# Ten of eleven f tiles of a gated feed-forward block's down product as 2x2 block products in seven, for half of the tokens

## The chip, the cores and the metric

The kernel runs on one core of one Trainium2 chip. The metric is the device time of one execution in microseconds. Engine names in the profile: PE is TensorE (PEld its weight loads), DVE is VectorE, ACT is ScalarE, POOL is GpSimd, SP the engine whose queue issues the transfers.

## The reference, cut to what matters

A transformer block with adaptive layer norm, linear attention and a bilinear feed-forward part, 2048 tokens of 512 features, all in float32:

```
h = layernorm(x) * (1 + ca) + sa
x = x + ga * linear_attention(h, wqkv) @ wo
h = layernorm(x) * (1 + cb) + sb          # 2048 x 512
g = h @ w_gate                            # 2048 x 1376
u = h @ w_up                              # 2048 x 1376
x = x + gb * ((g * u) @ w_down)           # w_down: 1376 x 512
```

The change is in the last three lines.

## The kernel before

The tokens are four chunks of 512. In the feed-forward part two chunks make a side: side 0 is chunks 0 and 1, side 1 is chunks 2 and 3. The 1376 columns of w_gate and w_up are eleven f tiles (ten of 128, the last of 96). The loop over `order` runs 22 blocks: all f tiles of side 0, and then all of side 1. The f tiles are in five groups, `groups`: four of two and a last of three.

A number is carried as two float32r parts, a high one and a low one (`split`: ScalarE copies the high part, another engine subtracts). A product then takes three matmuls: high by high, high by low, low by high. A float32r matmul loads 128x128 weights and streams up to 512 columns into one PSUM bank.

One block computes, for its f tile, gate and up of both chunks as a product of 2x2 blocks (chunks by halves of the features, halves of the features by gate and up) with seven products instead of eight, in Winograd's form. `block` (line 984) writes them in a fixed order with `times` (line 965): seven products of 6 matmuls of 512 columns, into four banks a, b, c and d that all blocks share. ScalarE's `copy` carries a partial sum from bank to bank between the products: after b has its product with s2, b goes to c; after c has its product with s3, c is copied into u3, which VectorE adds to d; the product with a22 then goes on top in c. At the end VectorE multiplies gate by up (`product_of`, line 994) and gets two tiles h, one for each chunk; `todo` holds the splits of these, which run in the next block behind its second product (`flush`). `at` is a table of work that the loop puts at named points between the products: a11, s1, s2, s3, pe, mid, s4. The engines run their instructions in the order in which the program issues them, and an instruction that waits holds all behind it on its engine. All transfers are issued on SP's queue, in order.

The right side of a block, `Right` (line 921), is loaded from w_gate and w_up, three blocks ahead; GpSimd makes the differences that the seven products need (`sums`), ScalarE the high parts and GpSimd the low parts (`high`, `lows`). It is made anew for each side. The left side of side 1 is prepared during side 0 and kept in DRAM (`aside`, `fetch`).

The down product (`down`, line 1039) of a group runs in the blocks of the next group. A job takes two token tiles (of the four of a chunk), and for each of them 3 matmuls of 512 columns for each f tile of the group, into a bank of the pool `ps_acc` (4 banks); VectorE adds the bank to the token tile in `xts` (line 1055). The jobs stand at the point pe, between the products with s3 and with a22; their adds are issued at s4. The jobs of the last group of side 1 have no block behind them: one job of four token tiles and four of one are issued after the last block, each add followed by the store of its tile of the output. w_down's rows are scaled by gb on VectorE (`scale_down`) and split (`split_down`).

All working tiles, 2 KB in each partition, are from one pool of 99 (`B`); the program's order decides which place a new tile gets, and whose last use it waits for.

Of the kernel before, what the change touches and what calls it, by code (L numbers as in the profile page):

```python
# [22 lines left out]
def tile_adaln_block(  # L23
# [41 lines left out]
    def f32(ap):  # L65
        return ap.bitcast(F32)
# [7 lines left out]
    def B(tag, shape=(P, D), dt=F32):  # L74

        return T(tiles, tag, shape, dt)
# [313 lines left out]
    sums = {}  # L390
# [522 lines left out]
    def fetch(stash, side, *names):  # L913
        for n in names:
            side[n] = []
            for k in range(KH):
                side[n].append(tuple(B("h", dt=F32R) for _ in range(2)))
                for part, x in enumerate(side[n][k]):
                    nc.sync.dma_start(f32(x), stash[n, k, part])

    class Right:
# [24 lines left out]
        def high(self):  # L946
            self.parts = []
            self.b11 = self.tile("w", F32R)
            nc.scalar.activation(self.b11[:, 0], self.up[:, 0], AF.Copy)  # L949
            for names, x in ((("t1", "t2"), self.t12), (("b21", "b22"), self.low), (("t3", "t4"), self.t34)):  # L950
                h = self.tile("w", F32R)
                nc.scalar.activation(h, x, AF.Copy)
                self.parts.append((names, x, h))

        def lows(self, on=None):
            sub = lambda out, x, y: (on or nc.gpsimd).tensor_tensor(out, x, f32(y), op=ALU.subtract)  # L956
            self.of = {"b11": (self.b11[:, 0], self.b11[:, 1])}
            sub(self.b11[:, 1], self.up[:, 0], self.b11[:, 0])
            for names, x, h in self.parts:
                l = self.tile("w", F32R)  # L960
                sub(l, x, h)
                for i, name in enumerate(names):
                    self.of[name] = (h[:, i], l[:, i])

    def times(ps, left, right, fresh):

        (bh, bl) = right
        for k in range(KH):
            ah, al = left[k]
            mm = lambda x, y, **kw: nc.tensor.matmul(ps, x[:, k], y, skip_group_check=True, **kw)  # L970
            mm(bh, ah, start=fresh and k == 0, stop=False)
            mm(bh, al, start=False, stop=False)
            mm(bl, ah, start=False, stop=k == KH - 1)

    def copy(out, x):
        nc.scalar.activation(out, x, AF.Copy)  # L976
# [4 lines left out]
        while todo:  # L981
            todo.pop(0)()

    def block(A, R, at={}, end=False):


        n, R = R.n, R.of
        a, b, c, d = (x[:n] for x in (abank, bbank, cbank, dbank))
        out = [None, None]

        def also(point):
            run(at.get(point, ()))

        def product_of(i, x, y):
            t = B("phi")
            nc.vector.tensor_tensor(t[:n], x, y, op=ALU.mult)  # L996

            def halves():
# [23 lines left out]
        nc.vector.tensor_tensor(c22[:n], d, u3[:n], op=ALU.add)  # L1022
# [12 lines left out]
        rest()  # L1035
        also("s4")
        return out

    def down(ch, hs, ds, js=range(NJ), last=False):
# [17 lines left out]
                    nc.sync.dma_start(ov[ch, j], xt)  # L1057
        return take

    def load_down(f):  # L1060
        f0, n = fts[f]
        return load(w_down[f0:f0 + n, :], "raw")

    def scale_down(d):
        nc.vector.tensor_tensor(d, d, gb[:d.shape[0]], op=ALU.mult)
# [3 lines left out]
    order = [(s, g, f) for s in range(2) for g in range(len(groups)) for f in groups[g]]  # L1069
    rights = {}  # L1070

    def right_load(n):
        if n < len(order):
            rights[n] = Right(order[n][2])

    def right_sums(n, on=None):
        if n < len(order):
            rights[n].sums(on)

    def right_split(n, on=None):  # L1080
        if n < len(order):
            rights[n].high()
            rights[n].lows(on)

    side, stash, lefts = {}, {}, {}

# [111 lines left out]
    }  # L1198

    before = None  # L1200
    for n, (s, g, f) in enumerate(order):
        first, final = f == groups[g][0], f == groups[g][-1]
        if first:
            if before is not None:
                down_jobs(*before)
            for x in groups[g]:
                raw_d[s, x] = load_down(x)
        at = {p: list(early.get((n, p), ())) for p in ("a11", "s1", "s2", "s3", "mid", "s4", "pe")}
        taken = []
        after = len(groups[g]) - groups[g].index(f)  # L1210
        for _ in range(-(-len(fillers) // after)):
            job = fillers.pop(0)
            at["pe"].append(lambda job=job: taken.append(job()))
            at["mid" if n + 1 == len(order) else "s4"].insert(0, lambda: taken.pop(0)())
# [12 lines left out]
        at["s3"] += [lambda n=n: right_load(n + 3)]  # L1227
        at["s4"] += [lambda n=n: right_sums(n + 2), lambda d=raw_d[s, f]: scale_down(d)]
        if n:
            at["s2"].insert(0, lambda s=order[n - 1][0], f=order[n - 1][2]: split_down(s, f))  # L1230
        if s == 0 and n == 9:
            after_side = {}
            at["pe"].append(lambda: fetch(stash, after_side, "a11", "a12"))
# [5 lines left out]
        hs[s, f] = block(side, rights.pop(n), at=at)  # L1239
# [11 lines left out]
_INS = ["A_x", "A_wqkv", "A_wo", "B_w_gate", "B_w_up", "B_w_down", "c", "w_mod"]  # L1251
# [24 lines left out]
```

## Time and profile before

| | us |
|---|---|
| median of 3 runs | 563.58 (562.93 to 564.28) |
| profiled execution, its own time | 561.47 |
| its span, first to last instruction | 559.8 |

| engine | busy us | share of the span | instructions |
|---|---|---|---|
| PE | 551.9 | 99% | 2544 |
| DVE | 379.8 | 68% | 648 |
| ACT | 294.2 | 53% | 531 |
| POOL | 207.4 | 37% | 226 |

Transfers read 43.12 MB from and wrote 13.63 MB to DRAM. The blocks of side 1 begin about 384 us from the span's start.

In the rows of the profile, a group is one line of the kernel on one engine: what it writes and reads, the tiles' sizes, the count, then busy time and the mean duration of one in ns, and the idle time before it with who ended it. A row of a timeline begins with the start and the duration in us. A row of a stretch has its bounds and length, then PE, PEld, DVE, ACT and POOL busy with their counts, the granted clock, the share of the transfer engines and GB/s. Matmuls overlap: their durations add up to more than the time they take.

### The profile page before, as it was taken

To read this page: it belongs to the slowest core of one execution; us is meant where nothing else is said; L and a number is where in the kernel's file an instruction comes from. 1 tells how busy PE (TensorE), PEld (TensorE's weight loads), DVE (VectorE), ACT (ScalarE), POOL (GpSimd) and SP (SyncE) were. 2 spreads that over 40 slices of the span, in tenths; PEclk is the share of its full clock that TensorE was granted. 3 is DMA by queue.
4 is the path that set the end of the run, shared out by engine and by line. 5 is a ranking of instruction groups with operands and counts; after the bars stand their busy time and mean duration, and the time that the engine had idled before them with its cause. 6 is when DMAs were issued, how large, how long until landed. Compare 5 with 4: busy or idle time off the path is not lost.

```text
span 559.8 us, 7391 instructions
## 1 busy us (share of the span) xinstructions
PE 551.9 (99%) x2544; PEld 453.5 (81%) x2544; DVE 379.8 (68%) x648; ACT 294.2 (53%) x531; POOL 207.4 (37%) x226
## 2 busy tenths in 40 slices
PE   7999999999999999999999999999999999999997
PEld 5888888888888888888888888878888888888775
DVE  5968779869898998865655766862455545444653
ACT  3876858446476877663545355553444334334420
POOL 2000000003327646343556644485424455554200
PEclk9999999999999999999999999999999999999999
DMA  8910224202230020151446136598353211200004
GB/s 254 384 39 1 75 76 150 77 0 71 80 114 2 0 76 0 39 159 68 150 151 195 32 122 221 178 363 286 114 157 87 57 39 48 71 0 1 0 1 150
DMA packets 50133, 57.24 MB, mean 102 GB/s; under 512 B 6384, under 2 KB 28912, under 8 KB 50096
## 3 DMA queue, kind: packets, MB, share of 16 engines
q1 hardware_dynamic: 50096, 56.77, 31.8%
q8 instruction: 20, 0.33, 0.3%
q14 instruction: 17, 0.14, 0.1%
HBM read 43.12 MB, written 13.63 MB: 101 GB/s over the span
## 4 chain that ended last, share of the span: by engine, by line
PE 94%; DVE 3%; DMA 1%; SPq 0%; issue 0%; ACT 0%; POOL 0%
PE bank L970 38%; PE acc L807 8%; PE acc L1048 7%; PE acc L1049 7%; PE acc L1050 7%; PE bank L206 5%; PE bank L207 5%; PE bank L208 5%; PE acc L357 2%; PE acc L355 2%; PE acc L356 2%; PE bank L271 2%; PE acc L439 1%; DMA x<-in_A_x_dram 1%; PE bank L782 1%; PE acc L271 1%
## 5 line engine op out<-in xcount | busy, mean ns | idle before, releaser
L970 PE MATMUL bank<-h,w 128*128 128x512 f32 (+1 forms) x924 | 215.8, 390 | 0.0
L970 PEld LDWEIGHTS bank<-h,w 128*128 128x128 f32 (+1 forms) x924 | 170.8, 185 | 38.6 <-issue 0.4
L976 ACT ACTIVATE bank<-bank 128x512 f32<-128x512 f32 (+1 forms) x44 | 25.6, 581 | 151.2 <-PE bank L970 151.1
L956 POOL TENSOR_TENSOR w<-raw,w 128x256 fp32r<-128x256 f32 (+3 forms) x44 | 46.1, 1048 | 157.2 <-ACT w L949 150.0
L996 DVE TENSOR_TENSOR phi<-bank,g 128x512 f32<-128x512 f32 (+1 forms) x22 | 15.1, 688 | 83.5 <-PE bank L970 79.8
L1048 PE MATMUL acc<-w,kh 128*128 128x512 f32 (+1 forms) x176 | 68.6, 390 | 0.0
L1049 PE MATMUL acc<-w,kh 128*128 128x512 f32 (+1 forms) x176 | 68.6, 390 | 0.0
L1050 PE MATMUL acc<-w,kl 128*128 128x512 f32 (+1 forms) x176 | 68.5, 389 | 0.0
L956 POOL TENSOR_TENSOR w<-t,w 128x512 fp32r<-128x512 f32 (+1 forms) x44 | 57.4, 1305 | 0.0
L1055 DVE TENSOR_TENSOR x<-acc,x 128x512 f32<-128x512 f32 x80 | 50.3, 681 | 8.6 <-PE acc L1050 8.6
L206 PE MATMUL bank<-w,h 128*128 128x512 f32 x112 | 44.8, 400 | 0.0
L208 PE MATMUL bank<-w,h 128*128 128x512 f32 x112 | 43.7, 390 | 0.0
L207 PE MATMUL bank<-w,h 128*128 128x512 f32 x112 | 43.6, 390 | 0.0
L676 POOL TENSOR_TENSOR f<-h,zb 128x512 f32<-128x512 f32 x12 | 17.1, 1439 | 67.8 <-ACT zb L656 49.2
L249 POOL TENSOR_TENSOR rstd<-ve,half 128x4 f32<-128x4 f32 (+3 forms) x12 | 11.2, 930 | 83.0 <-DVE ve L246 71.4
L807 PE MATMUL acc<-w,xh 128*128 128x512 f32 x128 | 40.7, 399 | 0.0
L1048 PEld LDWEIGHTS acc<-w,kh 128*128 128x128 f32 (+1 forms) x176 | 33.0, 188 | 7.1
L1050 PEld LDWEIGHTS acc<-w,kl 128*128 128x128 f32 (+1 forms) x176 | 33.0, 188 | 7.0
L1049 PEld LDWEIGHTS acc<-w,kh 128*128 128x128 f32 (+1 forms) x176 | 33.1, 188 | 6.9
L938 POOL TENSOR_TENSOR t<-raw,t 128x256 f32<-128x256 f32 (+1 forms) x44 | 36.9, 838 | 1.7
L1022 DVE TENSOR_TENSOR g<-bank,u 128x512 f32<-128x512 f32 (+1 forms) x22 | 15.2, 691 | 27.0 <-ACT u L976 27.0
L264 ACT ACTIVATE n<-x,nmr,rstd 128x512 f32<-128x512 f32 x31 | 23.7, 808 | 14.6 <-DVE nmr L254 14.4
(159 smaller groups left out, 1011.3 us busy)
## 6 DMA issues: line engine op xcount, KB each, us to landing
x<-in_A_x_dram SPq DMA_DIRECT2D x24, 256.0 KB, 5.2
raw<-in_w_mod_dram SPq DMA_DIRECT2D x24, 256.0 KB, 3.8
raw<-in_B_w_gate_dram SPq DMA_DIRECT2D x40, 128.0 KB, 3.0
raw<-in_B_w_up_dram SPq DMA_DIRECT2D x40, 128.0 KB, 3.1
raw<-in_B_w_down_dram SPq DMA_DIRECT2D x20, 256.0 KB, 3.1
side_s<-h SPq DMA_DIRECT2D x16, 256.0 KB, 2.5
h<-side_s SPq DMA_DIRECT2D x16, 256.0 KB, 5.5
out_dram<-x SPq DMA_DIRECT2D x16, 256.0 KB, 2.6
```

The lines of the kernel that those rows point to most:

```text
L206: nc.tensor.matmul(ps, ah, bh, start=i == 0, stop=False)
L207: nc.tensor.matmul(ps, ah, bl, start=False, stop=False)
L208: nc.tensor.matmul(ps, al, bh, start=False, stop=i == n - 1)
L807: nc.tensor.matmul(yps[i], x, y, start=fresh and k + n == 0, stop=k == KD - 1 and n == 2, skip_group_check=True)
L938: sub = lambda out, x, y: (on or nc.gpsimd).tensor_tensor(out, x, y, op=ALU.subtract)
L956: sub = lambda out, x, y: (on or nc.gpsimd).tensor_tensor(out, x, f32(y), op=ALU.subtract)
L970: mm = lambda x, y, **kw: nc.tensor.matmul(ps, x[:, k], y, skip_group_check=True, **kw)
L976: nc.scalar.activation(out, x, AF.Copy)
L1048: nc.tensor.matmul(dn[j], hh[:n, a:b], dh[:n], start=i == 0, stop=False)
L1049: nc.tensor.matmul(dn[j], hh[:n, a:b], dl[:n], start=False, stop=False)
L1050: nc.tensor.matmul(dn[j], hl[:n, a:b], dh[:n], start=False, stop=i == n_of - 1)
L1055: nc.vector.tensor_tensor(xt, dn[j], xt, op=ALU.add)
```

## The change

For side 1, the first two f tiles of each group become a pair. Their two h tiles for two chunks are a 2x2 block matrix, and the two f tiles' rows of w_down by the halves of its 512 columns another; their product is taken in seven block products in place of eight, again in Winograd's form. The outputs of each are 256 columns wide, two token tiles share a bank. Each of seven steps has 6 matmuls (two token tiles by three), and all but the first are followed by two adds of 256 columns on VectorE, into halves of two token tiles. ScalarE copies bank a to bank b once for each seven (`seed`). The f tile 10 keeps its down product as before, after the last block.

The sums and splits that this needs are new: on the left s1 to s4 from VectorE, high parts on ScalarE, low parts on VectorE (one on GpSimd); on the right GpSimd's differences and low parts (`weight_sums`, `weight_splits`).

The steps go into a queue, from which one is taken at each of seven points of a block (`POINTS`), behind each product, instead of whole jobs at pe. The pair's steps begin at pe of the block behind the pair. A point a12 is added in `block`, ahead of the product with s3. Four steps are left in the queue after the last block; they alternate with the seven of the last two token tiles (in banks of the other pool), and then with the jobs of f tile 10.

The right sides are made once. Their seven tiles (256 KB each) are stored in DRAM in side 0's blocks, at a11 (those of the last two f tiles at s4 of side 1's first blocks), and side 1 loads them from there, two blocks ahead (`RightKept`), in place of the weights, sums and splits.

```diff
+        def keep(self, store):
+            for x in [self.b11] + [y for _, _, h in self.parts for y in (h, self.lows_of[id(h)])]:
+                store.append(tc.dram_tile([P, 2, KH, self.n], F32, name=f"right_{len(rights_kept)}_{len(store)}"))
+                nc.sync.dma_start(store[-1], f32(x))
+    class RightKept:
+        def __init__(self, f, store):
+            for x in store:
+                got.append(B("w", (P, 2, KH, self.n), F32R))
+                nc.sync.dma_start(f32(got[-1]), x)
...
     def block(...):
         copy(g[:n], a)
+        also("a12")
         times(c, A["s3"], R["t3"], False)
...
+    class Pair:
+        def sum(self, n, on):
+            x, y, alu = {"s1": ("a21", "a22", ALU.add), "s3": ("a11", "a21", ALU.subtract),
+                         "s2": ("s1", "a11", ALU.subtract), "s4": ("a12", "s2", ALU.subtract)}[n]
+            self.f[n] = B("s")
+            on.tensor_tensor(self.f[n], self.f[x], self.f[y], op=alu)
+        def first(self):
+            self.sum("s3", nc.vector)
+            self.split("a11", nc.vector)
+            self.split("s3", nc.vector)
+        def second(self):
+            for n in ("a22", "a12", "s1", "s2", "s4"):
+                if n[0] == "s":
+                    self.sum(n, nc.vector)
+                self.high(n)
+        def lows(self, *ns):
+            for n in ns:
+                self.low(n, nc.gpsimd if n == "a22" else nc.vector)
...
+        def product(self, ps, j, x, y, fresh):
+            (hh, hl), (dh, dl) = self.h[x], self.d[y]
+            a, b = j * P, (j + 1) * P
+            mm = lambda x, y, **kw: nc.tensor.matmul(ps, x[:, a:b], y, skip_group_check=True, **kw)
+            mm(hh, dh, start=fresh, stop=False)
+            mm(hh, dl, start=False, stop=False)
+            mm(hl, dh, start=False, stop=True)
+    def pair_steps(s, pair, js, of=acc_bank):
+        xa, xb = ([xts[c][j] for j in js] for c in sides[s])
+        halves = slice(0, HD), slice(HD, D)
+        def step(b, x, y, to, at, fresh=False, then=None):
+            if fresh:
+                banks[b] = of()
+            for m, (part, j) in enumerate(zip(halves, js)):
+                pair.product(banks[b][:, part], j, x, y, fresh and m == 0)
+            if then:
+                then()
+            for part, xt in zip(halves, to):
+                nc.vector.tensor_tensor(xt[:, halves[at]], banks[b][:, part], xt[:, halves[at]], op=ALU.add)
+        def seed():
+            banks["b"] = of()
+            copy(banks["b"], banks["a"])
+        return [lambda: step("a", "a11", "b11", (), 0, True, seed),
+                lambda: step("d", "s1", "t1", xb, 1, True),
+                lambda: step("b", "s2", "t2", xa, 1),
+                lambda: step("a", "a12", "b21", xa, 0),
+                lambda: step("b", "s3", "t3", xb, 1),
+                lambda: step("d", "s4", "b22", xa, 1),
+                lambda: step("b", "a22", "t4", xb, 0)]
...
+    POINTS = ("a11", "s1", "s2", "a12", "pe", "mid", "s4")
...
+        if s == 0:
+            keeps.append((f, rights[n]))
+        if n < NF - 2:
+            at["a11"] += [lambda: right_keep(*keeps.pop(0))]
+        elif n in (NF, NF + 1):
+            at["s4"] += [lambda: right_keep(*keeps.pop(0))]
         at["s3"] += [lambda n=n: right_load(n + 3)]
+        at["s4" if s else "s3"] += [lambda n=n: right_back(n + 2)]
...
+            if n > NF + 1 and f in pair_of and first:
+                queue += [x for js in ((0, 1), (2, 3)) for x in pair_steps(1, pairs[g - 1], js)]
+            if f == tail:
+                queue += pair_steps(1, pairs[g], (0, 1))
...
+            for p in POINTS[4:] if n == NF + 2 else POINTS:
+                at.setdefault(p, []).append(lambda: queue and queue.pop(0)())
...
     flush()
-    split_down(1, order[-1][2])
-    down_jobs(*before)
-    for job in fillers:
-        job()()
+    split_down(1, tail)
+    more = pair_steps(1, pairs[len(groups) - 1], (2, 3), of=bank)
+    rest = lambda c, *js: down(sides[1][c], [hs[1, tail][c]], [split_d[1, tail]], js, True)()
+    while queue:
+        queue.pop(0)()
+        more.pop(0)()
+    rest(0, 0, 1)
+    more.pop(0)()
+    rest(1, 0, 1)
+    while more:
+        more.pop(0)()
+    rest(0, 2, 3)
+    rest(1, 2, 3)
```

More of the change, by code (lines that the diff above doesn't have):

```diff
@@ L961, in lows @@
                 sub(l, x, h)
+                self.lows_of[id(h)] = l
+                for i, name in enumerate(names):
+                    self.of[name] = (h[:, i], l[:, i])
+        def keep(self, store):
[4 more added lines that the diff above has]
+        def __init__(self, f, store):
+            self.n = fts[f][1]
+            got = []
+            for x in store:
+                got.append(B("w", (P, 2, KH, self.n), F32R))
+                nc.sync.dma_start(f32(got[-1]), x)
+            b11, parts = got[0], got[1:]
+            self.of = {"b11": (b11[:, 0], b11[:, 1])}
+            for m, names in enumerate((("t1", "t2"), ("b21", "b22"), ("t3", "t4"))):
+                h, l = parts[2 * m:2 * m + 2]
                 for i, name in enumerate(names):
@@ L982, in flush, with block @@
             todo.pop(0)()
-    def block(A, R, at={}, end=False):
+    def block(A, R, at={}, done=None):
         n, R = R.n, R.of
@@ L996, in product_of @@
             nc.vector.tensor_tensor(t[:n], x, y, op=ALU.mult)
+            if done:
+                done(i, t)
+                return
             def halves():
@@ L1070, in tile_adaln_block, with right_back, right_keep @@
     rights = {}
+    rights_kept = {}
     def right_load(n):
-        if n < len(order):
+        if n < NF:
             rights[n] = Right(order[n][2])
+    def right_back(n):
+        if NF <= n < len(order) and n not in rights:
+            rights[n] = RightKept(order[n][2], rights_kept[order[n][2]])
     def right_sums(n, on=None):
-        if n < len(order):
+        if n < NF:
             rights[n].sums(on)
     def right_split(n, on=None):
-        if n < len(order):
+        if n < NF:
             rights[n].high()
             rights[n].lows(on)
+    def right_keep(f, right):
+        store = rights_kept[f] = []
+        right.keep(store)
     side, stash, lefts = {}, {}, {}
@@ L1200, in tile_adaln_block @@
     before = None
+    pairs = {}
+    queue, keeps = [], []
+    tail = groups[-1][-1]
+    POINTS = ("a11", "s1", "s2", "a12", "pe", "mid", "s4")
+    pair_of = {f: g for g, fs in enumerate(groups) for f in fs[:2]}
+    weights = {}
     for n, (s, g, f) in enumerate(order):
@@ L1203, in tile_adaln_block @@
         if first:
-            if before is not None:
+            if before is not None and before[0] == 0:
                 down_jobs(*before)
-            for x in groups[g]:
+            for x in groups[g] if s == 0 else ():
                 raw_d[s, x] = load_down(x)
@@ L1213, in tile_adaln_block @@
             at["pe"].append(lambda job=job: taken.append(job()))
-            at["mid" if n + 1 == len(order) else "s4"].insert(0, lambda: taken.pop(0)())
+            at["mid" if s else "s4"].insert(0, lambda: taken.pop(0)())
         if s == 0 and n == 3:
@@ L1238, in tile_adaln_block, with done @@
             at["s2"].insert(0, lambda: fetch(stash, after_side, "a22", "s4"))
-        hs[s, f] = block(side, rights.pop(n), at=at)
+        done = None
+        if s == 1 and f in pair_of:
+            at_first = f == groups[g][0]
+            if at_first:
+                pairs[g] = Pair()
+                at["pe"].append(lambda xs=groups[g]: raw_d.update({(1, x): load_down(x) for x in xs}))
+                sums = lambda g=g, x=groups[g]: pairs[g].weight_sums(raw_d[1, x[0]], raw_d[1, x[1]])
+                if g:
+                    at["mid"].insert(0, sums)
+            else:
+                if not g:
+                    at["s2"].append(sums)
+                at["s3"] += [lambda g=g: pairs[g].weight_splits(0, 2)]
+                at["mid"] += [lambda g=g: pairs[g].weight_splits(1, 3)]
+            def done(i, t, p=pairs[g], at_first=at_first):
+                p.f[(("a11", "a21") if at_first else ("a12", "a22"))[i]] = t
+                if i == 0:
+                    todo.append(p.first if at_first else p.second)
+        if s == 1:
+            if n > NF + 1 and f in pair_of and first:
+                queue += [x for js in ((0, 1), (2, 3)) for x in pair_steps(1, pairs[g - 1], js)]
+            if f == tail:
+                queue += pair_steps(1, pairs[g], (0, 1))
+            if first and g:
+                at["s2"].append(lambda p=pairs[g - 1]: p.lows("s1", "s2"))
+                at.setdefault("a12", []).append(lambda p=pairs[g - 1]: p.lows("a12", "s4", "a22"))
+            elif f == tail:
+                at["s2"].append(lambda p=pairs[g]: p.lows("s1", "s2"))
+                at.setdefault("a12", []).append(lambda p=pairs[g]: p.lows("a12", "s4", "a22"))
+            for p in POINTS[4:] if n == NF + 2 else POINTS:
+                at.setdefault(p, []).append(lambda: queue and queue.pop(0)())
+        hs[s, f] = block(side, rights.pop(n), at=at, done=done)
         if final:
```

42 lines of the change are left out of this document (40 added, 2 removed).

## The prediction

> **What bounds the kernel now.** I read the page's first part, then what TensorE waited for, then the busy time by stretch.
>
> ```profile
> span 559.8 us, 7391 instructions
> PE 551.9 (99%) x2544; PEld 453.5 (81%) x2544; DVE 379.8 (68%) x648; ACT 294.2 (53%) x531; POOL 207.4 (37%) x226
> ...
> PE acc L153 <- DVE w L148: 2.0, 1, 2.0
> PE bank L278 <- ACT n L264: 1.0, 2, 0.6
> ...
> 420.00:467.00 47.00, 47.00 (x209) 38.94 (x208) 22.69 (x36) 18.58 (x36) 24.07 (x27) 1.00 0.24 65
> 512.00:539.10 27.10, 27.10 (x120) 21.15 (x119) 16.08 (x25) 10.58 (x21) 5.70 (x8) 1.00 0.00 1
> 539.10:559.80 20.70, 16.63 (x73) 13.35 (x71) 9.29 (x14) 1.42 (x3) 0.00 (x0) 1.00 0.29 102
> ```
>
> TensorE (PE) is busy in 551.9 of 559.8 us and its waits come to a few us, all near the start. In the second pair of chunks (the stretches after 384 us) it is busy without a gap at a granted clock of 1.00, while VectorE (DVE) is busy 22.69 of 47.00 us. So an edit pays only by TensorE time, and loses by whatever makes TensorE wait. The price of one matmul is its pitch, start to start; its duration (0.39) contains a tail that overlaps the next.
>
> ```profile
> 422.08 9.52 PE bank L970 x42
> 437.04 9.52 PE bank L970 x42
> ...
> 539.12 0.39 PE L1048 MATMUL acc<-w,kh 128*128 128x512 f32 x1
> ...
> 555.77 0.69 DVE x L1055
> ...
> 138.08 0.27 PE L208 MATMUL bank<-w,w 128*128 128x128 f32 x1
> ...
> 141.43 0.28 PE L208 MATMUL bank<-w,w 128*128 128x128 f32 x1
> ...
> 138.13 0.19 PEld L206 LDWEIGHTS bank<-w,w 128*128 128x128 f32 x1
> 138.24 0.19 PEld L207 LDWEIGHTS bank<-w,w 128*128 128x128 f32 x1
> ```
>
> The first two rows are from the chain that ended last: two blocks of the second half, 14.96 us apart. A block is 42 matmuls of its own (9.52, or 0.2267 each) and 24 of the down products. 539.12 is the first matmul behind the last block's own products, 555.77 the last add. The other rows are the only stretch with narrower outputs: from 138.08 to 141.43 are 30 steps, 0.1117 each, for 128 columns. There the weight loads stand 0.11 apart too.
>
> **The change, TensorE's sum.** A pair of f tiles took 2 x 8 x 3 = 48 matmuls of 512 columns. It now takes 7 products x 4 token tiles x 3 = 84 of 256 columns. For five pairs, 240 go and 420 come; the 24 of the last f tile stay. Removed: 240 x 0.2267 = 54.4 us. Added: 420 x p, and no row shows p, the pitch at 256 columns. Below, it is bounded by 0.1117 (a load is still needed for each) and by half of the 512 pitch, 0.1134; above, by the straight line from 0.1117 at 128 to 0.2267 at 512 columns, 0.150. At 128 columns the loads run as close as the matmuls, so that row is a load's pitch rather than a stream's, and the line through it is too steep. I take 0.120, nearer to the half pitch, with 6 ns for load and stream now being equally long, so that neither covers the other's fixed part. Then 420 x 0.120 = 50.4: 4.0 us less. Break-even is 54.4 / 420 = 0.1295.
>
> The Trainium skill (TensorE: Matmul & The Clock Gate, LDWEIGHTS) speaks against narrow outputs: a load takes its number of columns / 1.2 GHz, 107 ns here, however few columns stream past it, and its fast load is not had for FP32. Its section on the back-to-back gap gives 256 / 2.4 + 2.5 = 109 ns for the stream. By that page p would be about 0.109 and the matmuls 8.6 us less, an estimate; the trace agrees on the load (0.11) and is above its 216 ns at 512 columns (227), so I don't go as low.
>
> **Where these matmuls stand.** The order of the built program puts the steps (6 matmuls each) behind the block's own products: 3 steps in the third block of the second half, 7 in each of the eight after it, and 11 steps after the last block. Take T0, the end of the last block's own products: 539.1. Of the 420, 72 come behind it (one step stands behind the last product) and 348 before it; of the removed 240 and kept 24, 192 stood before it and 72 behind. So T0 moves by 348 x 0.120 - 192 x 0.2267 = 41.8 - 43.5 = -1.8.
>
> **A wait that the change adds.** Before, a whole down job stood between the product that adds s3 and the one that adds a22 to bank c, and hid ScalarE's copy of the bank (u3).
>
> ```profile
> 446.40 0.39 PE L1048 MATMUL acc<-w,kh 128*128 128x512 f32 x1
> ...
> 446.60 0.60 ACT L976 ACTIVATE u<-bank 128x512 f32<-128x512 f32 x1 [0.63 <-PE bank L970]
> ...
> 447.23 0.69 DVE L1022 TENSOR_TENSOR g<-bank,u 128x512 f32<-128x512 f32 x1 [1.16 <-ACT u L976]
> ```
>
> The copy's reader starts 447.23 - 446.40 = 0.83 after the first matmul behind the product. The cover is now one step, 6 x 0.120 = 0.72. TensorE waits 0.11 in each of nine blocks, and with it all that is queued behind: +1.0. The other hand-overs in a block have one product and two steps, 1.36 + 1.44 = 2.8 us, against a copy of 0.6 or an add of 0.69; they cost nothing as long as VectorE and ScalarE aren't behind.
>
> **VectorE.** This is the cover that could go.
>
> ```profile
> L1055 DVE TENSOR_TENSOR x<-acc,x 128x512 f32<-128x512 f32 x80 | 50.3, 681 | 8.6 <-PE acc L1050 8.6
> L194 DVE TENSOR_TENSOR kl<-phi,kh 128x512 fp32r<-128x512 f32 x40 | 26.7, 708 | 0.0
> L996 DVE TENSOR_TENSOR phi<-g,g 128x512 f32<-128x512 f32 x20 | 15.5, 776 | 1.1
> L1065 DVE TENSOR_TENSOR raw<-raw,row 128x512 f32<-128x512 f32 x20 | 14.3, 714 | 0.0
> L171 DVE SCALAR_TENSOR_TENSOR f<-raw,sc,f 128x512 f32<-128x512 f32 x12 | 9.0, 750 | 0.3
> L889 DVE TENSOR_TENSOR s<-f,f 128x512 f32<-128x512 f32 x6 | 5.3, 910 | 3.1 <-DMA f<-kept 3.1
> L171 DVE SCALAR_TENSOR_TENSOR f<-raw,sc,f 128x256 f32<-128x256 f32 x9 | 4.4, 484 | 0.3
> ...
> 441.19 2.48 DVE L1055 TENSOR_TENSOR x<-acc,x 128x512 f32<-128x512 f32 x4
> ```
>
> The 256-column add from PSUM is not in the trace. The two L171 rows differ by 0.266 for 256 columns, which makes it 0.681 - 0.266 = 0.415; 0.484 is the upper bound. The heavier block of each pair (the first) has, by durations, 4 operations of its own (0.69 x 3 + 0.78 = 2.85), 12 adds (4.98), 3 sums (at 0.776, 2.33), 4 low parts (2.83) and 2 scalings (1.43): 14.4 us. The block takes 9.52 + 42 x 0.120 + 0.11 = 14.67. The lighter one has 2.85 + 4.98 + 0.78 + 1.42 = 10.0. But four such operations take 2.48, not 2.72: starts stand 0.60 apart, some 0.08 inside the duration. With 25 operations that is 2 us of room in the heavier block. I cost VectorE at nothing in the blocks.
>
> **The end.** Before, the last add started at 555.77 and ended 0.69 later, 17.3 behind T0. Now TensorE has 72 x 0.120 + 24 x 0.2267 = 14.1, and VectorE, at starts 0.60 and (0.60 - 0.266) 0.334 apart: the last two of the block's own and a low part chain to about 4.0, then 20 small adds (6.7) and 8 full ones (4.8), 15.5 in all. Worked in order, with TensorE held twice for an add of the same bank (0.1 and 0.9), both end together: the last add at 15.6. That is -1.7. Eight outputs now leave in one burst rather than 2.06 apart, the last four 0.6 apart; I add 0.3, guessed between nothing and one landing (2.6, below).
>
> **Copies of the rights.** Seven tiles of 256 KB per f tile are stored and fetched again: 19.7 MB each way; the weights are no longer read a second time.
>
> ```profile
> DMA  8910224202230020151446136598353211200004
> GB/s 254 384 39 1 75 76 150 77 0 71 80 114 2 0 76 0 39 159 68 150 151 195 32 122 221 178 363 286 114 157 87 57 39 48 71 0 1 0 1 150
> ...
> h<-side_s SPq DMA_DIRECT2D x16, 256.0 KB, 5.5
> out_dram<-x SPq DMA_DIRECT2D x16, 256.0 KB, 2.6
> ```
>
> A block stores 1.84 MB in 15 us, 120 GB/s beside up to 363; in the second half it fetches as much where 39 to 157 flowed. On SP, seven stores stand at each block's start and wait for GpSimd's last low part; behind them are the loads of the rights three blocks on, the kept tiles and the fetches. The order with its waits gives each fetched right 72 matmuls or more, over 12 us, against a landing of 5.5, so I cost this at nothing; without that cover it would be one landing. GpSimd (24.07 busy in 47.00) and ScalarE (18.58) lose the splits of the rights in the second half and get back those of the pairs; neither was on the path.
>
> **Sum.** -1.8 + 1.0 - 1.7 + 0.3 = -2.2. The profiled execution took 561.47 (559.8 and 1.7 around it), 2.1 under the median of 563.58; on the median the forecast is 561.4. A change under 0.2% (1.1 us) can't be told from none.
>
> **The rivals.**
> A, the narrow matmul runs at its floor, 0.1117: T0 moves 38.9 - 43.5 + 9 x (0.83 - 0.67) = -3.2, the end -2.2, +0.3: 558.5. For it: the loads at 0.11. Against it: half of the 512 pitch, 0.1134, is already above it. The Trainium skill's gap formula, cited above, is on its side. Chance 0.12.
> B, slower: VectorE, in order, sets the pace in the heavier block of a pair. Price: adds at 0.484 (5.81) and the seven sums and low parts at 0.91 (6.37, the L889 row) with 2.85 and 1.43 make 16.5, 1.8 more than 14.67, in four blocks: +7.3, 568.7. It decides where that block's VectorE work passes 14.7 us. Against: starts 0.60 apart. Chance 0.18, with it a late right or copy of a few us.
> C, the straight line, 0.150: T0 moves 52.2 - 43.5 = +8.7 with no u3 wait, the end nearly as before (+0.3): 572.6. Chance 0.10.
> D, the change does less than it says: the removed work wasn't on the path. No: the windows have PE without a gap. The remaining 0.05 is for what I don't see.
>
> **How the numbers follow.** The forecast's case has 0.55 and runs from p = 0.1134 (-4.5: 559.1) to 0.126 (563.6, near no change). Chances: faster 0.38 of it (p under 0.1226) and A, 0.50; same 0.14 of it, 0.03 of B and 0.02, 0.19; slower the rest, 0.31. The range holds the case, most of A and B to its price, and leaves out C: 558.8 to 568.7.
>
> **What would show it.** The pitch within a step (12 matmuls in 1.44); 14.67 between blocks from the fourth of the second half on; TensorE's waits on ScalarE's u copies at 0.11 each; VectorE near 85% in the heavier block with TensorE not waiting for its adds; the last add 15.6 behind the last block's products. A pitch over 0.126, or waits on DVE over 2 us in sum, makes the forecast wrong.

## The result, and the profile after

| | median us | against before |
|---|---|---|
| before, 20 runs | 562.91 (560.85 to 564.65) | |
| after, 20 runs | 565.00 (563.19 to 567.19) | 1.0042, 95% interval 1.0029 to 1.0054 |
| forecast | 561.4 (558.8 to 568.7) | faster |

The change makes the kernel 2.1 us slower. The forecast had the wrong sign. That the time is inside the range is luck: the range reached this far up for the price of rival B, a late VectorE, and that is not what happened. The profiled execution after took 566.3 us, with a span of 564.6.

The page's first part, and what TensorE's matmuls and weight loads waited for (us in total, times, longest), after:

```profile
span 564.6 us, 8045 instructions
PE 555.9 (98%) x2724; PEld 461.4 (82%) x2724; DVE 421.1 (75%) x756; ACT 294.9 (52%) x522; POOL 174.4 (31%) x183
...
PEld bank L993 <- DMA h<-side_s: 2.2, 6, 0.5
...
PEld bank L993 <- ACT u L999: 1.7, 9, 0.2
PEld bank L993 <- ACT bank L999: 0.9, 2, 0.7
...
PEld acc L1152 <- DVE x L1172: 0.4, 2, 0.2
```

TensorE is still busy nearly throughout. All four rows are new; before, the profile lists no wait of TensorE from 340 us on. They are the waits for the left side that is fetched at the edge between the halves (side_s), for ScalarE's copy u3 (line 999), nine times, for ScalarE's copies from bank to bank, twice, and for VectorE's adds. The last, which rival B stood on, come to 0.4 us, both behind the last block.

The chain that ended last, in two of the blocks of the second half, after (start, us, what):

```profile
495.94 1.63 PE bank L993 x6
497.57 0.71 PE acc L1152 x6
498.28 1.39 PE bank L993 x6
...
510.88 1.65 PE bank L993 x6
...
525.84 1.63 PE bank L993 x6
```

A step is 6 narrow matmuls in 0.71 to 0.72 us, 0.119 each: the 0.120 of the forecast. But the product with a22 (1.63) now stands 14.94 to 14.96 after that of the block before, just as far as before the change. The blocks were to be 14.67 apart. Each other product behind a step takes 1.39 where six matmuls took 6 x 0.2267 = 1.36. (Over six blocks, in the table below, the spacing is even 0.03 wider than before.)

Where the 4.8 us between the two spans arose is read from the start of ScalarE's copy g, which each block makes once; the blocks are counted from the program's first, and 12 is the first of the second half. T0 is the end of the last block's own products, as in the prediction.

| stretch | before | after | difference | forecast of it |
|---|---|---|---|---|
| start to g of block 10 | 356.59 | 358.25 | +1.66 | 0 |
| to g of block 13 (the edge) | 41.08 | 42.37 | +1.29 | 0 |
| to g of block 14 | 17.78 | 18.37 | +0.59 | 0 |
| to g of block 15 | 14.96 | 14.17 | -0.79 | 36 x 0.120 + 0.11 - 24 x 0.2267 = -1.0 |
| to g of block 21 (six blocks) | 89.76 | 89.91 | +0.15 | 6 x (14.67 - 14.96) = -1.7 |
| to g of block 22 | 12.34 | 14.91 | +2.57 | 42 x 0.120 + 0.11 - 12 x 0.2267 = +2.4 |
| to T0 | 6.61 | 6.54 | -0.07 | 18 x 0.120 + 0.11 - 12 x 0.2267 = -0.4 |
| T0 to the end of the last add | 17.34 | 15.41 | -1.93 | -1.7 |
| last add to the end of the span | 3.3 | 4.6 | +1.3 | +0.3 |

The first row is not the change's. The busy time by stretch (the figure behind the busy times is the granted clock), first before, then after:

```profile
0.00:60.00 60.00, 56.28 (x264) 46.12 (x265) 44.22 (x97) 37.75 (x60) 5.34 (x19) 1.00 0.47 159
```
```profile
0.00:60.00 60.00, 57.45 (x257) 47.20 (x258) 44.24 (x97) 36.19 (x58) 5.34 (x19) 0.94 0.45 158
```

In the first 60 us both programs do the same, and this execution of after was granted 0.94 there where before had 1.00. Of the 1.66, 1.58 are there by the first copy g (218.40 and 219.98); from it to g of block 10, where the rights are stored, are 138.2 and 138.3 us. The clock differs from run to run (0.97 in most variants below), so traces are compared from g of block 10 on: 203.2 us from there to the end before, 206.3 after.

The edge, busy time by stretch; the last two figures are the share of the transfer engines and GB/s. First before, then after:

```profile
360.00:375.00 15.00, 15.00 (x67) 11.11 (x66) 9.22 (x12) 6.37 (x13) 12.33 (x13) 1.00 1.00 339
375.00:390.00 15.00, 15.00 (x67) 12.36 (x66) 5.67 (x8) 6.18 (x12) 10.37 (x11) 1.00 1.01 340
390.00:405.00 15.00, 15.00 (x68) 12.38 (x67) 7.56 (x12) 6.19 (x12) 5.20 (x6) 1.00 0.36 107
```
```profile
360.00:375.00 15.00, 15.00 (x67) 11.08 (x66) 8.22 (x14) 6.16 (x13) 3.93 (x4) 1.00 1.02 365
375.00:390.00 15.00, 14.66 (x61) 10.77 (x60) 7.32 (x12) 4.32 (x8) 0.00 (x0) 1.00 1.05 384
390.00:405.00 15.00, 15.00 (x68) 12.38 (x67) 7.34 (x11) 6.00 (x11) 5.03 (x6) 1.00 1.04 375
```

After, the transfer engines are full for all of these 45 us, in which the left side has to come; before, for 30 of them. The forecast read the 39 to 157 GB/s of the late slices as room; in the slices just ahead of them, where the left side is fetched, there was none.

### The profile page after: what moved, and what is told of

The parts are those of the page before. It is cut to its first block, busy times and chain, and to the rows that moved or that the text cites. A ratio compares the mean times of both kernels' runs of the same rounds, so it can differ in the third digit from the quotient of the medians.

```text
span 564.6 us, 8045 instructions
## 1 busy us (share of the span) xinstructions
PE 555.9 (98%) x2724; PEld 461.4 (82%) x2724; DVE 421.1 (75%) x756; ACT 294.9 (52%) x522; POOL 174.4 (31%) x183
## 4 chain that ended last, share of the span: by engine, by line
PE 93%; DVE 3%; DMA 2%; ACT 0%; issue 0%; SPq 0%; POOL 0%
PE bank L993 36%; PE acc L1152 8%; PE acc L807 8%; PE bank L206 5%; PE bank L207 5%; PE bank L208 5%; PE acc L1075 4%; PE acc L1076 4%; PE acc L1077 4%; PE acc L357 2%; PE acc L355 2%; PE acc L356 2%; PE acc L439 2%; PE bank L271 2%; DMA h<-side_s 1%; PE bank L782 1%
## 5 line engine op out<-in xcount | busy, mean ns | idle before, releaser
L993 PE MATMUL bank<-h,w 128*128 128x512 f32 (+1 forms) x924 | 227.7, 394 | 0.7 <-DMA h<-side_s 0.3
L1172 DVE TENSOR_TENSOR x<-acc,x 128x256 f32<-128x256 f32 x108 | 40.0, 415 | 20.3 <-PE acc L1152 20.3
L956 POOL TENSOR_TENSOR w<-raw,w 128x256 fp32r<-128x256 f32 (+3 forms) x22 | 24.2, 1100 | 77.1 <-ACT w L949 62.3
L1152 PE MATMUL acc<-w,kh 128*128 128x256 f32 x252 | 47.9, 283 | 0.0
L1152 PEld LDWEIGHTS acc<-w,kh 128*128 128x128 f32 x252 | 43.0, 190 | 5.4 <-DVE x L1172 0.4
L1082 DVE TENSOR_TENSOR x<-acc,x 128x512 f32<-128x512 f32 x48 | 30.5, 680 | 9.7 <-PE acc L1077 9.7
L1075 PE MATMUL acc<-w,kh 128*128 128x512 f32 (+1 forms) x96 | 37.5, 391 | 0.0
L1076 PE MATMUL acc<-w,kh 128*128 128x512 f32 (+1 forms) x96 | 37.5, 391 | 0.0
L1077 PE MATMUL acc<-w,kl 128*128 128x512 f32 (+1 forms) x96 | 37.4, 389 | 0.0
L1152 PE MATMUL acc<-w,kl 128*128 128x256 f32 x126 | 35.6, 283 | 0.0
L1019 DVE TENSOR_TENSOR phi<-bank,g 128x512 f32<-128x512 f32 (+1 forms) x22 | 15.1, 684 | 26.4 <-PE bank L993 24.9
L999 ACT ACTIVATE u<-bank 128x512 f32<-128x512 f32 (+1 forms) x44 | 26.1, 594 | 15.5 <-PE bank L993 15.5
```

Of the source, the lines that this page charges most:

```text
L1075: nc.tensor.matmul(dn[j], hh[:n, a:b], dh[:n], start=i == 0, stop=False)
L1076: nc.tensor.matmul(dn[j], hh[:n, a:b], dl[:n], start=False, stop=False)
L1077: nc.tensor.matmul(dn[j], hl[:n, a:b], dh[:n], start=False, stop=i == n_of - 1)
L1082: nc.vector.tensor_tensor(xt, dn[j], xt, op=ALU.add)
L1152: mm = lambda x, y, **kw: nc.tensor.matmul(ps, x[:, a:b], y, skip_group_check=True, **kw)
L1172: nc.vector.tensor_tensor(xt[:, halves[at]], banks[b][:, part], xt[:, halves[at]], op=ALU.add)
```

## The experiments

Three theories stood against each other. W: small waits between TensorE's products eat each block's gain. T: the rights' trips through DRAM cost the time. V: VectorE is late. Each variant was timed beside before on one chip, but not all variants on the same one, so they are best compared by their ratios to before; "W" below always means this theory.

**Two steps at pe (u3).** The cover of the copy u3 is doubled.

```diff
-    POINTS = ("a11", "s1", "s2", "a12", "pe", "mid", "s4")
+    POINTS = ("a11", "s1", "s2", "pe", "pe", "mid", "s4")
```

> The changed kernel with two steps at the point pe and none at a12, so that 12 narrow matmuls (1.43 us) instead of 6 (0.72) cover ScalarE's copy of bank c. Theory W (the gain of each block is eaten by small waits between the products: 0.24 us for the copy u3, and 0.03 at each change from 256 to 512 columns): the wait of 0.24 goes from nine blocks, and one change of width less: blocks 14.72 apart instead of 14.98, time 2.2 to 2.4 us under the changed kernel (562.7 where it has 565.0). Theory T (the transfers of the kept rights cost the time): nothing changes in the blocks' pace beyond the wait's 0.11 that was predicted, so 1.0 us at most. Theory V (VectorE is late in the heavier blocks): the wait only moves to another product, no change.

Measured: 562.52, 0.9997 of before (0.9974 to 1.0020). Against the ratio of the changed kernel, 1.0042, this is 0.0045, or 2.5 us. The chain, a block of it and the rows a block later:

```profile
503.63 2.77 PE bank L993 x12
506.41 1.43 PE acc L1152 x12
507.84 1.39 PE bank L993 x6
...
518.34 2.75 PE bank L993 x12
521.09 1.43 PE acc L1152 x12
```

Blocks are 14.68 apart, and the wait on u is not among TensorE's waits after 420 us. W holds, V does not: with the same work on VectorE the wait is gone rather than moved. The wait's price in the changed kernel is read from this place of its timeline:

```profile
509.55 0.62 PE L993 MATMUL bank<-h,w 128*128 128x512 f32 x2
...
510.00 0.40 PE L1152 MATMUL acc<-w,kh 128*128 128x256 f32 x2
...
510.20 0.60 ACT L999 ACTIVATE u<-bank 128x512 f32<-128x512 f32 x1 [1.44 <-PE bank L993]
...
510.83 0.69 DVE L1049 TENSOR_TENSOR g<-bank,u 128x512 f32<-128x512 f32 x1
510.86 0.53 PEld L993 LDWEIGHTS bank<-h,w 128*128 128x128 f32 x3 [0.18 <-ACT u L999]
510.86 0.74 PE L993 MATMUL bank<-h,w 128*128 128x512 f32 x2
```

The reader on VectorE starts 0.83 behind the product's end, as forecast, and TensorE goes on at 0.86, 0.14 late. But it is the weight load that has waited, and its 0.11 now stands in front of the matmul instead of under the one before: the first two matmuls take 0.74, where two without a wait (the first row) take 0.62. So 0.14 + 0.12 is about the 0.24 that the product is longer (1.63 for 1.39).

**Steps in pairs (group).** The seven steps stand at four points.

```diff
+    POINTS = ("s1", "s1", "a12", "a12", "pe", "pe", "s4")
```

> The changed kernel with its seven steps of a block at four points (two behind the second product, two at a12, two at pe, one at the block's end) instead of seven points. Theory W: the wait for u3 (0.24) goes, and of seven changes from 256 to 512 columns in a block, 0.03 us each, three go: blocks 14.65 apart, 0.33 less than the changed kernel's 14.98; 3.0 us less in nine blocks, 0.8 less than the variant with two steps at pe alone. Rival: a change of width costs nothing by itself, and the 1.39 of a product behind a step is the records' modelled end: then as the variant with two steps at pe, 2.2 less. Theory V: two steps in a row put four adds on VectorE at once and TensorE waits for a bank: no gain or slower.

Measured: 563.97, 1.0020 (0.9998 to 1.0042): 1.0 under the changed kernel, not 3.0. The chain:

```profile
501.42 2.75 PE bank L993 x12
504.17 1.43 PE acc L1152 x12
...
518.81 1.43 PE acc L1152 x12
...
525.92 0.70 DVE g L1058
526.82 1.57 issue
528.39 0.74 DVE x L1172 x2
...
537.21 0.99 PE acc L1152 x6
```

Blocks are 14.64 apart, as W had it: the two changes of width that go, beyond the one that the variant before already saved, take 0.02 to 0.03 each. It is no wait at the seam, nor the modelled end of a record, for the starts of the matmuls show it: the first five pitches of a product behind a step are 0.229 to 0.235 in this trace, the sixth and the six of the product behind it 0.227. Why is open; the width alone isn't it, for pitches of 0.229 to 0.235 also follow a wait in block 14 that has no narrow matmul ahead of it (in the trace with nine rights kept, below). The time doesn't show the gain. In the last block the chain leaves TensorE for VectorE at 525.9 (in the variant with two steps at pe only at 540.7), a step takes 0.99, and from the last copy g to the end are 27.3 us instead of 26.4. Here V has a point, in this one block. Whether the variant is slower than the one with two steps at pe is open: the intervals overlap, and from g of block 10 on both traces take 203.4 to 203.5.

**Rights made anew (nokeep).** The pairs stay, the copies in DRAM go. The edit, shortened:

```diff
+    KEPT = ()
     def right_load(n):
-        if n < NF:
+        if n < NF or n < len(order) and order[n][2] not in KEPT:
...
     def right_keep(f, right):
+        if f not in KEPT:
+            return
```

> The changed kernel with the rights made anew in the second half, as before the change: no copies in DRAM; GpSimd and ScalarE do the rights' differences and splits beside the pairs'. Theory T: the left side's fetch at the edge comes in time, 1.3 us less, and the later right copies no longer hold anything: 1.3 to 2 us under the changed kernel, 563.0 to 563.7. Theory W: the 1.3 at the edge only, with the blocks still 14.98 apart. Rival G: GpSimd (10.5 us of rights' work in each block beside the pair's low parts and differences) becomes late, rights arrive late, and TensorE waits: slower than the changed kernel by 3 us or more. The transfers fall from 161 to about 102 GB/s in the mean.

Measured: 575.54, 1.0227 (1.0199 to 1.0256), the time of rival G. Busy time by stretch, first with the rights made anew, then in the changed kernel:

```profile
435.00:544.00 109.00, 103.17 (x564) 85.92 (x563) 93.65 (x145) 55.75 (x106) 99.32 (x84) 1.00 0.13 35
```
```profile
435.00:544.00 109.00, 108.97 (x612) 93.33 (x612) 84.33 (x160) 48.34 (x86) 35.16 (x32) 1.00 0.32 102
```

GpSimd is busy 99.3 of 109 us and the blocks are 16.5 apart. So T is right only at the edge: there this variant is 0.2 faster than before, and the 1.3 are gone. But TensorE doesn't wait for late rights, as G had it. From 405 us on none of its waits is for GpSimd; the longest are for VectorE's adds:

```profile
PEld acc L1152 <- DVE x L1172: 4.7, 8, 0.8
...
PEld bank L993 <- DVE g L1049: 4.1, 3, 1.4
```

Why VectorE is late is seen in the same stretch's groups, first with the rights made anew, then in the changed kernel:

```profile
L1172 DVE TENSOR_TENSOR x<-acc,x 128x256 f32<-128x256 f32 x78 | 28.6, 411 | 10.3 <-PE acc L1152 10.3
L1101 DVE TENSOR_TENSOR kl<-s,kh 128x512 fp32r<-128x512 f32 x12 | 14.3, 1215 | 0.0
L1191 DVE TENSOR_TENSOR raw<-raw,row 128x512 f32<-128x512 f32 x6 | 8.7, 1480 | 0.0
```
```profile
L1172 DVE TENSOR_TENSOR x<-acc,x 128x256 f32<-128x256 f32 x86 | 31.9, 415 | 18.6 <-PE acc L1152 18.6
L1101 DVE TENSOR_TENSOR kl<-s,kh 128x512 fp32r<-128x512 f32 x15 | 10.0, 686 | 0.3
L1019 DVE TENSOR_TENSOR phi<-g,g 128x512 f32<-128x512 f32 x7 | 8.6, 1231 | 0.2
...
L1191 DVE TENSOR_TENSOR raw<-raw,row 128x512 f32<-128x512 f32 (+1 forms) x7 | 4.5, 683 | 0.0
```

Beside a busy GpSimd the operations whose inputs are both in SBUF take about twice as long, and the adds that read PSUM don't. GpSimd is slowed too: the pairs' low parts (line 1144) take 1641 and 1582 ns instead of 1293 and 1292. By these rows, the copies in DRAM pay for the pairs by keeping GpSimd out of VectorE's way.

**Only the copies (onlykeep).** Before's down products, with the rights kept in DRAM (`keep`, `RightKept` and `right_back` as in the change).

> The kernel before with one part of the change: the rights kept in DRAM and fetched in the second half; the down products stay as before. Theory T: the copies cost by themselves, 1.3 us or more at the edge (the left side's fetch waits among the rights' fetches): 564.2 or more where before has 562.9. Theory W: the edge's 1.3 at most and nothing else; the pace of the blocks stays at 14.96. Rival: the edge costs only because of other work that the changed kernel has there, then no difference from before (within 0.3 us).

Measured: 563.97, 1.0023 (1.0004 to 1.0043): T, and no more than the edge: blocks 14.96 apart. TensorE's timeline at the edge, first here, then in the changed kernel:

```profile
379.53 3.01 PE L993 MATMUL bank<-h,w 128*128 128x512 f32 x12 [0.15 <-DMA h<-side_s]
383.77 0.73 PE L993 MATMUL bank<-h,w 128*128 128x512 f32 x2 [1.22 <-DMA h<-side_s]
```
```profile
379.89 3.33 PE L993 MATMUL bank<-h,w 128*128 128x512 f32 x12 [0.16 <-DMA h<-side_s]
383.41 0.73 PE L993 MATMUL bank<-h,w 128*128 128x512 f32 x2 [0.18 <-DMA h<-side_s]
```

The copies alone cost 1.3 us in the median (0.2 to 2.4). In this one trace the edge costs 2.7 (g of block 10 to g of block 13), in the changed kernel's 1.3, with two steps at pe 0.5 and with the steps in pairs 0.6: its size differs from one execution to the next.

**Nine of eleven rights kept (edge).** Two steps at pe; the first two rights of the second half are made anew.

The edit is that of the rights made anew, with another list of what is kept:

```diff
-    KEPT = ()
+    KEPT = groups[1] + groups[2] + groups[3] + groups[4]
```

> The variant with two steps at pe, and the first two rights of the second half made anew (kept are nine of eleven), so that two fetches of 1.8 MB fall away just where the left side is fetched. Theory T (the left side comes late among the rights' fetches): the 0.54 us that this variant lost between the tenth and the thirteenth block goes, and perhaps the 0.6 of the block after it; 0.5 to 1.1 under the variant with two steps at pe (561.4 to 562.0 where it has 562.5). Rival: the loss there comes from the rest of the change (the rights' stores, the pair's own loads): then no difference, or slower by GpSimd's extra work.

Measured: 561.78, 0.9979 (0.9961 to 0.9996), faster than before; against the variant with all rights kept (0.9997) it is 1.0 us, with intervals that overlap. From g of block 10 to g of block 13 are 41.13 us, before's 41.08, and TensorE no longer waits for side_s. The theory holds at the edge in this trace, though 0.4 of the 0.5 come back in block 15 (14.52 for 14.16 from g to g), where TensorE waits for VectorE. The 0.6 of the block behind the edge stay. There, with no steps yet ahead of pe, the product with s3 waits 0.26 for ScalarE's copy of bank c, behind the pair's five high parts, and u3 has one step of cover. That product's first matmul starts 0.65 behind the one ahead of it and the second 0.33 behind the first, where 0.23 is usual: TensorE loses 0.5.

**Low parts on GpSimd behind the last block (tailpool).** Two steps at pe, and:

```diff
-                split(t[:n], h[:n], l[:n])
+                split(t[:n], h[:n], l[:n], last_low[0])   # nc.gpsimd behind the last block
...
-    flush()
     split_down(1, tail)
+    flush()
```

> The variant with two steps at pe, and three low parts behind the last block (two of h, one of w_down, 0.60 us each on VectorE) on GpSimd. Theory: behind the last block VectorE is busy without a gap from 540.0 to 556.1 and sets the end; 1.8 us of its work go, TensorE's 14.1 and its waits take over: the last add 0.8 to 1.5 earlier, the time 0.8 to 1.5 less. Rival: TensorE's end or the burst of eight outputs sets the time: last add earlier by 0.5 at most and no change in the time.

Measured: 563.45, 1.0019 (0.9999 to 1.0038). The theory fell. The last add ends 22.56 behind the last copy g instead of 21.66. VectorE, GpSimd and TensorE there:

```profile
543.68 1.83 DVE L1020 TENSOR_TENSOR phi<-g,g 96x512 f32<-96x512 f32 x1
```
```profile
543.67 1.29 POOL L194 TENSOR_TENSOR kl<-phi,kh 96x512 fp32r<-96x512 f32 x1 [1.65 <-PE acc L1153]
```
```profile
546.23 0.51 PE L1153 MATMUL acc<-w,kh 128*128 128x256 f32 x2 [1.16 <-DVE x L1173]
```

VectorE's product, 0.69 elsewhere, took 1.83 beside GpSimd's 1.29, the adds behind it were late, and TensorE waited 1.16 for one.

**Fewer stores at the end (nostore, onestore).** Two steps at pe; of the eight stores at the end the first four are left out, then three of the last four.

```diff
-                if last:
+                if last and j > 1:                              # nostore
+                if last and (j < 2 or (ch, j) == (3, 3)):       # onestore
```

> The variant with two steps at pe, without the stores of the first four of the last eight output tiles (and of those alone; these tiles of the output are left out). Theory: the last tiles leave in a burst behind each other, and 4.8 us from the last add to the span's end instead of 3.34 before come from that; with four stores of 256 KB left, 3.4 to 3.9, so 0.9 to 1.4 less. Rival: the last four alone, 0.6 apart, make it: no change (within 0.3).

> The variant with two steps at pe, without the stores of three of the last four output tiles (and of those alone, which are left out of the output); the last tile is still stored, alone in its 2 us. Theory, after the first four stores were shown to have no part in it: the last four stores of 256 KB, issued 0.6 us apart, need 0.7 us each of all transfer engines and queue behind each other; with one alone, 3.3 to 3.6 from the last add to the span's end instead of 4.8. Rival: the 4.8 has another cause (a slower landing for each store here): stays at 4.4 or more.

Measured: 563.26, 1.0007 (0.9987 to 1.0027), and 561.91, 0.9985 (0.9963 to 1.0008). VectorE's last adds and the stores in the trace, first without the first four, then without three of the last four (spans 559.3 and 560.2):

```profile
552.02 2.55 DVE L1082 TENSOR_TENSOR x<-acc,x 128x512 f32<-128x512 f32 x4
...
552.73 2.20 SPq L1084 DMA_DIRECT2D out_dram<-x  x4
```
```profile
554.03 2.54 DVE L1082 TENSOR_TENSOR x<-acc,x 128x512 f32<-128x512 f32 x4
```

From the last add to the end are 4.7 us without the first four stores, against 4.8 with all in the variant that this one is made from, and 3.7 with the last tile's store alone. So the last four, 0.6 us apart, make most of the 1.3 us, and no part of the earlier ones shows. The size is less sure: in the other traces with all eight stores and the last four 0.6 apart the stretch is 4.3 to 4.6 (the changed kernel's 4.6 among them), so the burst costs 0.6 to 1.1 over one store alone.

**Together (both, best).** Both group the steps in pairs (the last block as with two steps at pe) and make the first two rights anew; the first also has the low parts on GpSimd.

> All together: the steps grouped by two (in the last block as in the variant with two steps at pe), the first two rights made anew, the three last low parts on GpSimd. Theory: 0.05 less in each of seven blocks than the variant with two steps at pe, 0.5 to 1.1 at the edge and 0.8 to 1.5 at the end: 1.7 to 2.9 under it, 559.6 to 560.8, and 2 to 3 under before. Rival: the gains at the end or at the edge don't show (as in their own runs); then 562, no better than before.

> Steps grouped by two (in the last block as in the variant with two steps at pe) and the first two rights made anew; the low parts behind the last block on VectorE again. Theory: GpSimd's low parts cost 0.9 behind the last block in their own run (a VectorE operation of 0.69 took 1.83 beside one of them, and TensorE waited 1.2 for an add); without them the last add is 21.7 behind the last block's copy g instead of 22.6, so 0.5 to 0.9 under the version with all three: 560.5 to 560.9, about 2.3 under before. Rival: in the grouped order VectorE is later at the end anyway, and nothing is won: 561.4.

Measured: 561.38, 0.9973 (0.9958 to 0.9988), and 561.21, 0.9972 (0.9951 to 0.9993). The first is 1.4 under the variant with two steps at pe by the ratios (1.1 by the medians) instead of 1.7 to 2.9; in its trace the low parts on GpSimd brought a loss (the last add ends 22.55 behind the last copy g) rather than 0.8 to 1.5. In the second the last add ends 21.67 behind the last copy g, as expected, but its median is 0.2 lower instead of 0.5 to 0.9, which doesn't tell the two apart. It is 1.6 us faster than before (0.4 to 2.8). Its trace also limits the theory of the edge: with nine rights kept, TensorE still waits once for side_s, its load 0.9, and the edge costs 0.6; in the first's trace there is no such wait and it costs 0.2.

## Why the prediction was wrong

**The narrow matmul's price was right.** 0.119 for the 0.120 taken; rivals A (0.1117) and C (0.150) are out. The formula of the Trainium skill (TensorE: Matmul & The Clock Gate, back-to-back issue gap) gave an estimate of 109 ns; the trace is 10 ns above it.

**The u3 wait was mis-sized: 0.24, not 0.11, nine times, +1.2 us.** The mechanism, the place and the 0.83 were right. The term took the reader's delay for the wait, and left out that a load which waits can't run under the matmul ahead of it. Doubling the cover took 2.5 us away, the whole wait and one change of width.

**A term was missing: 0.03 for the product behind each step, about 1.5 us.** The sum multiplied each width by its own pitch; 58 times before T0 a 512-column product now follows 256-column matmuls (0.026 each by the starts of the matmuls). Pairing the steps showed it: 14.68 to 14.64 for two changes fewer. In six blocks these two terms make 6 x (0.13 + 7 x 0.026) = 1.9, which is the -1.7 that the blocks were to bring and did not.

**"I cost this at nothing" was wrong at the edge: +1.3 in the changed kernel's trace, 1.3 in the median of the copies alone.** That step compared a block's mean stores with a free peak, and gave the landing of a fetched right as the risk. The late transfer was not a right, but the left side, queued among them on transfer engines that were already full there before. With nine of eleven kept it is gone in two traces of three; in the third one wait stays and costs 0.6, and why is open.

**The end: -1.7 came, +0.3 was +1.3.** The last add ends 15.41 behind T0 where 15.6 was forecast, with VectorE busy without a gap up to it. The burst was guessed below one landing; four stores of 256 KB, 0.6 apart, cost 0.6 to 1.1 more than one alone. Of the two holds of TensorE that the forecast worked out (0.1 and 0.9), the trace has two of 0.2.

**"As long as VectorE and ScalarE aren't behind" did not hold in block 14: +0.6.** The forecast put the other hand-overs at nothing on this condition. In block 14 ScalarE is behind, with the pair's five high parts, and both the copy of bank c and u3 are late.

**The sum.** 1.2 + 1.5 + 1.3 + 1.0 + 0.6, less 0.2 that the end brought beyond its -1.7, is 5.4. From g of block 10 on the traces differ by +3.1 where -2.2 was forecast, which is 5.3. In the medians the difference is +2.1, 1.0 less than in these two traces. Why is not shown; at the edge alone the traces with the pairs and all rights kept differ by 0.8 (it costs 0.5 to 1.3 there). Neither of the two signs that were to make the forecast wrong appeared, a pitch over 0.126 or waits on VectorE over 2 us: what failed were smaller terms beside them.

**VectorE "at nothing" held in the blocks, though not by its own working.** Its operations beside GpSimd's were up to 1231 ns in the mean rather than 776, and it still hid. In the heavier blocks VectorE is busy 80% of the time. That GpSimd "was not on the path" held only because the rights are kept: made anew they cost 10.5 us more, by way of VectorE.

With the two steps at pe and nine rights kept, a part of the forecast's gain (2.2) is there: 1.2 us (0.2 to 2.2), 1.6 with the steps in pairs (0.4 to 2.8).

## What to carry to other kernels

When a wide unit of work is split to fill several gaps, recount each hand-over that it used to hide: a wait at TensorE costs the late copy plus a weight load. Price a change of shape at the seam as well as in the stretch, and a new transfer in the stretch where the queue is fullest, asking what else is in that queue. An edit that loses by small waits can be mended: here one moved call turned +2.1 us into nothing, and with two rights fewer in DRAM the kernel is 1.2 us faster than before.

## What the runs showed of the hardware

- A weight load that waits for a semaphore is exposed: the product took 1.63 instead of 1.39 though the data were only 0.14 late.
- VectorE and GpSimd hinder each other: 1.83 for 0.69 beside one operation of 1.29, 1215 and 1480 ns for 686 and 683 beside a GpSimd busy 91% of the time, and no change (411 to 415) for adds that read PSUM. The Trainium skill (SBUF — State Buffer, two separate sides) says that a VectorE operation with two inputs in SBUF and a GpSimd operation that reads SBUF exclude each other; the trace agrees: GpSimd's operation starts 0.01 ahead, and VectorE's ends 0.55 behind its end, about one start-to-start (0.60). With the rights made anew GpSimd's operations of 1293 ns took 1641.
- A 512-column product behind 256-column matmuls takes 0.03 more than behind its own kind. The extra lies in its first five matmuls, 0.229 to 0.235 from start to start instead of 0.227. Why is open; the same pitches follow a wait with no narrow matmul ahead of it.
